# Shifting the SBUF addresses of matmul operands: distances of 64 and 96 bytes in place of 0 and 32

## The chip, the cores and the metric

The kernel runs on one core of a Trainium2 chip. TensorE (PE) multiplies; its weight loads are listed as PEld. VectorE (DVE), ScalarE (ACT) and GpSimd (POOL) do the elementwise work, and SyncE (SP) issues nearly all DMAs in order from one queue. The metric is device time in microseconds (us).

## The reference

Attention over pooled keys and values, and two gated MLP layers after it, all in float32:

```python
k_p = k.reshape(B, H, S//8, 8, D).mean(axis=3)      # B, H, S, D = 8, 8, 576, 64
v_p = v.reshape(B, H, S//8, 8, D).mean(axis=3)
attn = softmax(q @ k_p.T / sqrt(D)) @ v_p
x = attn                                            # as 4608 tokens x 512
h = x @ w_in                                        # 512 x 2048
x = (h * clip(h + 3, 0, 6) / 6) @ w_out             # first layer
g = x @ w_gate                                      # 512 x 1536
out = (g * sigmoid(g) * (x @ w_val)) @ w_out2       # second layer
```

## The kernel before

Every large product is computed from operands that are split into a high part (rounded to the type float32r) and a low part (the rest). Three matmuls, high x high, high x low and low x high, stand for one product of float32. Each matmul loads its own stationary operand: 128 columns of 4 bytes, 512 bytes in each partition. The next matmul's load runs beside the stream of the moving operand of the matmul before.

There are four large products, in this order of time:

- first layer, up (L623 in `mm3`, 1728 matmuls of 512 columns): moving `x`, stationary `wu`. It goes over nine blocks of 512 tokens and 16 slices of the weights, twelve matmuls each; between two such groups the matmuls of the next block's attention are put in (L424 to L604).
- first layer, down (L891 in `down_b`, 3024 matmuls of 256 columns): moving `gb`, stationary `pw`. It goes over nine blocks, and in each over seven products (a Strassen scheme: sums of quarters on VectorE, seven products in place of eight), 48 matmuls each.
- second layer, up (L712 in `mm3x`, called from `up2`, 3024 matmuls of 384 columns): moving `xc`, stationary `wr`. Six groups of 768 tokens, in each 12 slices of the weights with seven products.
- second layer, down (L712 from `down2`, 2268 matmuls of 256 columns): moving `wr`, stationary `gc`.

The weights of the second layer go through a ring of four buffers (`ring_tile`, tag `wr`), which SP fills by DMA in the order of use (L691 for up). Pools are given out in a stack from the left and one from the right of SBUF; where a new pool lies over the bytes of an old one, its first writer waits for the last users of the bytes. The order of all instructions is the order of the code.

The operands' addresses in a partition, in bytes, as the pools give them out, and their remainders modulo 256. All offsets inside these tiles, of slices that a matmul reads, are multiples of 256, so that the remainder of a tile is the remainder of each operand in it:

| Tile | Before | mod 256 | After | mod 256 |
|---|---|---|---|---|
| `wu`; `pw` of products 3 to 6 in the same pool | 17088 | 192 | 17088 | 192 |
| `x`; `pw` of products 2 and 7 in the same pool | 82624 | 192 | 82688 | 0 |
| `gb` | 115424 | 224 | 115456 | 0 |
| `px`: `pw` of product 1 | 178112 | 192 | 178112 | 192 |
| `xc` (its first pool; the others alike modulo 256) | 206816 | 224 | 206816 + 160 | 128 |
| `wr` (ring) | 161760 | 224 | 160224 + 64 | 32 |
| `gc` | 53952 | 192 | 53952 | 192 |

Moving minus stationary operand, modulo 256, is thus before 0 in both up products and 32 in both down products. After it is 64 in the first layer's up, 64 in five of the seven products of its down and 0 in the other two (products 2 and 7, whose `pw` lies in the pool of `x`), and 96 in both products of the second layer.

Of the kernel before, what the change touches and what calls it, by code (L numbers as in the profile page):

```python
# [8 lines left out]
F32 = mybir.dt.float32  # L9
F32R = mybir.dt.float32r  # L10
# [13 lines left out]
def kernel(  # L24
# [28 lines left out]
    P = 128  # L53
# [15 lines left out]

    left_b, l1, l1_ps = ExitStack(), ExitStack(), ExitStack()  # L70
    wu_p = left_b.enter_context(tc.tile_pool(name="wu", bufs=4))
    x_p = left_b.enter_context(tc.tile_pool(name="x", bufs=2))
    gap_p = left_b.enter_context(tc.tile_pool(name="gap", bufs=1))
    gb_p = left_b.enter_context(tc.tile_pool(name="gb", bufs=4))
    t_p = l1.enter_context(tc.tile_pool(name="t", bufs=2))
    ps_y = l1_ps.enter_context(tc.tile_pool(name="ps_y", bufs=1, space=PSUM))
# [6 lines left out]

    ident = const.tile([P, P], F32, name="ident")
    half = const.tile([P, 1], F32, name="half")
    gap_p.tile([P, 8], F32, name="gap")

    BIG = 4096

# [10 lines left out]
    M = 384  # L100
# [47 lines left out]
    def split(hi, lo, src, lo_engine):  # L148
        nc.scalar.copy(out=hi, in_=src)  # L149
        lo_engine.tensor_tensor(out=lo, in0=src, in1=f32(hi), op=ALU.subtract)  # L150
# [58 lines left out]
    def sums_b(eng, v, ops=("T1", "T3", "T2", "T4")):  # L209
        for what in ops:  # L210
            a, b = {"T1": ("12", "11"), "T3": ("22", "12"), "T2": ("22", "T1"), "T4": ("21", "T2")}[what]
            eng.tensor_tensor(out=v(what), in0=v(a), in1=v(b), op=ALU.subtract)
# [6 lines left out]
    def new_q7(name):  # L219
        return q7_p.tile([P, 8 * WH], F32R, tag="q7", name=name)  # L220
# [433 lines left out]
    l2 = {}  # L654
    xc, ys, gf, gc, wr = {}, {}, {}, {}, {}
# [10 lines left out]
    def x_step(p, n, lo_eng, sum_eng):  # L666

        t = ys[p]
        place = {"11": 0, "T1": 0, "12": 1, "T3": 1, "21": 2, "T4": 2, "22": 3, "T2": 3}
        v = lambda what: t[:, place[what]]  # L670
        what, then = [("11", "T1"), ("22", "T3"), ("T1", "T2"), ("T2", None), ("21", "T4"), ("T4", None), ("T3", None)][n]
        if what == "11":
            x = new_q7("xc")[:, :4 * M].rearrange("p (a k n) -> p a k n", a=2, k=2)
        else:
            pool = l2["xa" if what in ("T1", "22") else "xt" if what == "T3" else "xb"]
            x = pool.tile([P, 2, 2, M], F32R, tag="x" + what, name="xc")
        xc[p, what] = x
        split(x[:, 0], x[:, 1], v(what), lo_eng)
        if then:
            sums_b(sum_eng, v, (then,))  # L680

    def ring_tile():
        return l2["ring"].tile([P, 2048], F32R, tag="wr", name="wr")

    def load_up(u):

        f, m = u
        src = s_up[f][m].rearrange("p s a k f -> p s (a k f)")
        for h, (a, b) in enumerate(((0, HALF), (HALF, 7))):
            t = ring_tile()  # L690
            nc.sync.dma_start(  # L691
                out=f32(t[:, :512 * (b - a)]), in_=src[:, a:b].rearrange("p s n -> p (s n)")
            )
            for s in range(a, b):
                wr["up", u, s] = t[:, 512 * (s - a):512 * (s - a + 1)].rearrange("p (a k f) -> p a k f", a=2, k=2)

    def load_dn(n):
        s = B7[DN[n][2]]
        src = s_dn[:, s].rearrange("p f a n -> p (f a n)")
        for h in range(2):  # L700
            t = ring_tile()
            k = NPAIR // 2 * 512
            nc.sync.dma_start(out=f32(t[:, :k]), in_=src[:, k * h:k * (h + 1)])
            for f in range(NPAIR // 2):
                wr["dn", n, NPAIR // 2 * h + f] = t[:, 512 * f:512 * (f + 1)].rearrange("p (a n) -> p a n", a=2)
# [236 lines left out]
    for j in range(NB):  # L942
        t0 = j * N
        while t0 < (j + 1) * N:
            b, s0 = t0 // S, t0 % S
            n = min(S - s0, (j + 1) * N - t0)
# [198 lines left out]
    with tc.manual_schedule():  # L1145
# [105 lines left out]
        for i in range(7 * NB):  # L1251
            j, n = divmod(i, 7)
            down_b(i)
            for c in range(NCB):
                if c % (NCB // 2) == 0 and sums_at.get(n, ((), ()))[c // (NCB // 2)]:
                    sum_b(j, *sums_at[n][c // (NCB // 2)])
                split_b(i + 1, c)
            for slot in {3: (0,), 4: (2,), 5: (3, 1)}.get(n, ()):
                load_g(j + 1, slot)
            if j == NB - 1 and n >= 5:  # L1260
                if n == 5:
                    right_b.close()
                    prep_ctx.close()
                    for nm, bufs in (("xa", 1), ("ring", 4), ("xb", 1)):
                        l2[nm] = ctx.enter_context(
                            tc.tile_pool(name=nm, bufs=bufs, side="right", reuse_waits="tile"))
                load_next()
                for step in ((0,), (1, 2, 3))[n - 5]:
                    x_step(0, step, nc.vector, nc.vector)
            evac_b(j, n)  # L1270
            prep_slot(F1 * (NB - 1) + i)
            if (j, n) == (NB - 1, 3):
                assert not prep_at
                load_y(0)
        for step in (4, 5):
            x_step(0, step, nc.vector, nc.vector)
        for send in last_y:
            send()
        left_b.close()
        l2["xt"] = ctx.enter_context(tc.tile_pool(name="xt", bufs=1, side="right", reuse_waits="tile"))  # L1280
        x_step(0, 6, nc.vector, nc.vector)
        for nm, bufs in (("gf", 1), ("gc", 6), ("t", 1), ("o", 1)):
            l2[nm] = ctx.enter_context(tc.tile_pool(name=nm + "2", bufs=bufs, reuse_waits="tile"))
# [59 lines left out]
```

## Time and profile before

| What | Value |
|---|---|
| Median of three runs | 1747.0 us (1746.58 to 1748.53) |
| The profiled execution's own time | 1755.87 us |
| Its span (first to last instruction) | 1753.7 us |
| PE busy | 1698.7 us, 97% of the span |
| DVE busy | 1335.5 us, 76% |
| Granted TensorE clock, mean | 0.988 of full |

The profiled execution is one run with the profiler on; 2.2 us of its time lie outside the span, and it is 8.9 us above the median of the runs without a profile. Matmuls are pipelined: the duration of one record is longer than the distance from its start to the next one's start. Where matmuls follow each other with no idle time, a stretch of time divided by their number gives that distance.

### The profile page before, as it was taken

Reading aid. Unit: us, or ns where it says so; the run is one execution under the profiler, and the core shown is the slowest. Engines: PE = TensorE matmul, PEld = TensorE weight load, DVE = VectorE, ACT = ScalarE, POOL = GpSimd, SP = SyncE. Lnnn points to the kernel's source line nnn. Section 1 sums busy time; section 2 is a strip of 40 time slices with the busy share of each in tenths; the row PEclk is TensorE's granted clock in tenths of the full one; section 3 lists DMA queues with packets and bytes.
Section 4 is the critical chain, followed back from the end, with each engine's and each line's share of the span. In section 5 each row is a group of like instructions: output and inputs, shape, how many; then the busy total and the mean of one; then the engine's idle time right before and its main releaser. Section 6 shows DMA issues by size and latency. Waiting matters only on the chain.

```text
span 1753.7 us, 30755 instructions
## 1 busy us (share of the span) xinstructions
PE 1698.7 (97%) x11116; PEld 1603.2 (91%) x11116; DVE 1335.5 (76%) x2356; ACT 752.3 (43%) x1656; POOL 639.8 (36%) x821
## 2 busy tenths in 40 slices
PE   5789999999999999999999999999999999999999
PEld 4678887878788899999998999999999999999999
DVE  6797897888975578888887668668668668668666
ACT  5565554545544445555554224224224224224223
POOL 6555675656822000000000560560560560560560
PEclk8799999999999999999999999999999999999999
DMA  7666888888767974655554878878868878878776
GB/s 182 165 177 191 241 268 252 247 266 241 229 234 263 413 290 169 186 205 217 207 207 167 285 241 279 309 240 279 309 240 280 308 240 281 307 241 281 271 240 217
DMA packets 237784, 432.48 MB, mean 247 GB/s; under 512 B 87104, under 2 KB 169024, under 8 KB 220480
## 3 DMA queue, kind: packets, MB, share of 16 engines
q1 hardware_dynamic: 236576, 430.25, 73.6%
q8 instruction: 88, 1.44, 0.3%
q14 instruction: 64, 0.52, 0.1%
q10 hardware_dynamic: 1056, 0.26, 0.1%
HBM read 326.11 MB, written 104.33 MB: 245 GB/s over the span
## 4 chain that ended last, share of the span: by engine, by line
PE 83%; DMA 6%; DVE 6%; POOL 1%; ACT 1%; SPq 1%; issue 1%; DVEq 0%; POOLq 0%; ACTq 0%
PE b L712 45%; PE b L891 20%; PE h L623 14%; DMA g<-g 2%; DMA q_in<-in_q_dram 2%; PE pss L503 1%; DMA qv<-in_q_dram 1%; DVE g L638 1%; DMA y<-o 1%; SPq L384 1%; PE pst L573 1%; PE pst L577 0%; DVE vtl L469 0%; PE psv L601 0%; DVE qT L485 0%
## 5 line engine op out<-in xcount | busy, mean ns | idle before, releaser
L712 PE MATMUL b<-xc,wr 128*128 128x384 f32 x3024 | 527.9, 335 | 4.5 <-ACT xc L149 2.6
L712 PEld LDWEIGHTS b<-xc,wr 128*128 128x128 f32 x3024 | 525.5, 188 | 5.8 <-ACT xc L149 3.3
L623 PE MATMUL h<-x,wu 128*128 128x512 f32 x1728 | 432.6, 402 | 6.3 <-DVE g L638 6.1
L759 POOL TENSOR_TENSOR s<-s,c 128x384 f32<-128x384 f32 x144 | 142.3, 1013 | 755.3 <-ACT s L757 755.3
L721 DVE TENSOR_TENSOR c<-c,b 128x384 f32<-128x384 f32 x504 | 264.8, 552 | 174.6 <-PE b L712 149.8
L623 PEld LDWEIGHTS h<-x,wu 128*128 128x128 f32 x1728 | 321.5, 192 | 73.1 <-DVE g L638 8.8
L891 PEld LDWEIGHTS b<-gb,pw 128*128 128x128 f32 x3024 | 356.3, 188 | 0.2
L891 PE MATMUL b<-gb,pw 128*128 128x256 f32 x3024 | 356.4, 280 | 0.0
L712 PE MATMUL b<-wr,gc 128*128 128x256 f32 x2268 | 265.6, 279 | 0.0
L712 PEld LDWEIGHTS b<-wr,gc 128*128 128x128 f32 x2268 | 265.4, 188 | 0.0
L149 ACT CAST gb<-gq 128x512 fp32r<-128x512 f32 x252 | 155.3, 621 | 159.3 <-PE b L891 140.6
L150 DVE TENSOR_TENSOR gb<-gq,gb 128x512 fp32r<-128x512 f32 x252 | 167.5, 687 | 53.1 <-ACT gb L149 52.4
L766 POOL TENSOR_TENSOR gf<-s,c 128x384 f32<-128x384 f32 x144 | 168.2, 1192 | 66.3 <-DVE c L721 64.5
L149 ACT CAST gc<-gf 128x768 fp32r<-128x768 f32 x126 | 105.6, 838 | 187.1 <-POOL gf L766 100.8
L757 ACT ACTIVATE s<-c 128x384 f32<-128x384 f32 x144 | 73.4, 525 | 198.4 <-DVE c L721 197.1
L150 DVE TENSOR_TENSOR gc<-gf,gc 128x768 fp32r<-128x768 f32 x126 | 134.2, 1093 | 16.2 <-ACT gc L149 14.0
L634 ACT ACTIVATE g<-h,half 128x512 f32<-128x512 f32 x144 | 98.9, 687 | 78.6 <-PE h L623 62.8
L638 DVE SCALAR_TENSOR_TENSOR g<-g,h 128x512 f32<-128x512 f32 x144 | 97.4, 677 | 24.4 <-ACT g L634 24.3
L551 POOL TENSOR_TENSOR e<-e,sm 128x288 f32<-128x288 f32 (+4 forms) x74 | 48.3, 653 | 128.0 <-DVE sm L547 100.2
L729 ACT COPY c<-b 128x384 f32<-128x384 f32 x72 | 33.9, 470 | 127.4 <-PE b L712 127.4
L869 DVE TENSOR_TENSOR gq<-gq 128x1024 f32<-128x1024 f32 x72 | 87.7, 1218 | 0.0
L207 DVE TENSOR_TENSOR gf<-gf 128x768 f32<-128x768 f32 (+1 forms) x66 | 66.9, 1029 | 12.2 <-POOL gf L766 10.9
(101 smaller groups left out, 1660.1 us busy)
## 6 DMA issues: line engine op xcount, KB each, us to landing
wr<-sup SPq DMA_DIRECT2D x72, 1024.0 KB
wr<-sdn SPq DMA_DIRECT2D x84, 768.0 KB
wr<-sup SPq DMA_DIRECT2D x72, 768.0 KB
g<-g SPq DMA_DIRECT2D x144, 256.0 KB
gq<-g SPq DMA_DIRECT2D x36, 1024.0 KB
wstg<-in_moe_w_out_dram SPq DMA_DIRECT2D x56, 256.0 KB
pw<-sw SPq DMA_DIRECT2D x14, 1024.0 KB
sup<-s SPq DMA_DIRECT2D x12, 1024.0 KB
```

Of the source, the lines that this page charges most:

```text
L149: nc.scalar.copy(out=hi, in_=src)
L150: lo_engine.tensor_tensor(out=lo, in0=src, in1=f32(hi), op=ALU.subtract)
L623: nc.tensor.matmul(out=ps, lhsT=w(kt, wh), rhs=x(kt, xh), start=first and n == 0, stop=last and n == 3 * len(kts) - 1,)
L634: nc.scalar.activation(out=t, in_=ps, func=ACTF.Relu, bias=half, scale=1.0 / 6.0)
L638: nc.vector.scalar_tensor_tensor(out=t, in0=t, scalar=1.0, in1=ps, op0=ALU.min, op1=ALU.mult)
L712: nc.tensor.matmul(out=ps, lhsT=w(wh), rhs=x(xh), start=first and n == 0, stop=last and n == 2)
L721: add = lambda dst, a, b: nc.vector.tensor_tensor(out=dst, in0=a, in1=b, op=ALU.add)
L757: nc.scalar.activation(out=g[q], in_=c[q], func=ACTF.Sigmoid)
L759: nc.gpsimd.tensor_tensor(out=g[q], in0=g[q], in1=c[q], op=ALU.mult)
L766: nc.gpsimd.tensor_tensor(out=gf[p][:, GP[TURN[q]], f], in0=g[q], in1=c[q], op=ALU.mult)
L869: nc.vector.tensor_tensor(out=v(what), in0=v(a), in1=v(b), op=op)
L891: nc.tensor.matmul(out=ps[:, d], lhsT=w[:, CB * c + k, wh, P * d:P * (d + 1)], rhs=g[:, gh, k], start=what == place and (c, d, k, m) == (0 ...
```

## The change

It moves tiles by some bytes. The dummy tile `gap`, 32 bytes between the pool `x` and the pool `gb`, becomes 64 bytes between the pool `wu` and the pool `x`. In the second layer the tiles of `xc` and of the ring get 64 elements (256 bytes) more, and the operands start 40 and 16 elements (160 and 64 bytes) into them. No instruction is added or removed, and the engines' orders are the same.

```diff
     wu_p = left_b.enter_context(tc.tile_pool(name="wu", bufs=4))
+    gap_p = left_b.enter_context(tc.tile_pool(name="gap", bufs=1))
     x_p = left_b.enter_context(tc.tile_pool(name="x", bufs=2))
-    gap_p = left_b.enter_context(tc.tile_pool(name="gap", bufs=1))
     gb_p = left_b.enter_context(tc.tile_pool(name="gb", bufs=4))
...
-    gap_p.tile([P, 8], F32, name="gap")
+    gap_p.tile([P, 16], F32, name="gap")
...
         if what == "11":
-            x = new_q7("xc")[:, :4 * M].rearrange("p (a k n) -> p a k n", a=2, k=2)
+            x = new_q7("xc")
         else:
             pool = l2["xa" if what in ("T1", "22") else "xt" if what == "T3" else "xb"]
-            x = pool.tile([P, 2, 2, M], F32R, tag="x" + what, name="xc")
-        xc[p, what] = x
+            x = pool.tile([P, 4 * M + 64], F32R, tag="x" + what, name="xc")
+        x = xc[p, what] = x[:, 40:40 + 4 * M].rearrange("p (a k n) -> p a k n", a=2, k=2)
...
     def ring_tile():
-        return l2["ring"].tile([P, 2048], F32R, tag="wr", name="wr")
+        return l2["ring"].tile([P, 2048 + 64], F32R, tag="wr", name="wr")[:, 16:16 + 2048]
```

The longer tiles move the pools of the right side, and with them what some first writers of the second layer wait for. On SP, at the passage from the first layer to the second (`wr` is the ring, `sup` the prepared weights in memory, `ystg` and `y` the first layer's result, DVE_49 and the like are semaphores), the waits of the first four loads of weights change:

```order
 L663 DMA ystg<-y 128x2x384 [waits DMAHW3_49]
 L663 DMA ystg<-y 128x2x384 [waits DMAHW4_49]
-L691 DMA wr<-sup_107 128x2048 [waits DMAHW5_49,DVE_49]
+L691 DMA wr<-sup_107 128x2048 [waits DMAHW5_49,DVE_49,Activation_49]
 L691 DMA wr<-sup_107 128x1536 [waits PE_49]
-L691 DMA wr<-sup_108 128x2048
+L691 DMA wr<-sup_108 128x2048 [waits DVE_49]
 L691 DMA wr<-sup_108 128x1536 [waits DMAHW0_49]
 L912 DMA y<-o_11512 128x2x256 [waits DMAHW1_49,DVE_49]
```

Before, the first ring buffer covered the first 32 bytes of the quarter `gq` of slot 1, whose last reader is the last split of `gb` on DVE (L150); that wait moves to the third load. The first load now waits for the sum of L869 on DVE before it, and for a cast of ACT (L149) before it, which read the quarters that the buffer lies over now.

On ACT, at the same place, the third row is the cast that fills the last `xc` of the first group (`xt`), which lies over other buffers of the first layer's output than before:

```order
 L149 CAST xc<-ystg 128x768 [waits DMAHW3_49]
 L149 CAST xc<-ystg 128x768 [waits DVE_49]
-L149 CAST xc<-ystg 128x768 [waits DMAHW2_49,DMAHW1_49]
+L149 CAST xc<-ystg 128x768 [waits DMAHW2_49,DMAHW6_49,DMAHW1_49,DMAHW0_49]
 L729 COPY c_11620<-b 128x384 [waits PE_49]
```

It waits for two more stores of that output (L912), and the subtraction on DVE behind it for one more. Nothing else differs on any engine, PE among them.

## Rows read from the trace of the kernel before

**Rows 1.** The page's first part: the span, and each engine's busy time.

```profile
span 1753.7 us, 30755 instructions
PE 1698.7 (97%) x11116; PEld 1603.2 (91%) x11116; DVE 1335.5 (76%) x2356; ACT 752.3 (43%) x1656; POOL 639.8 (36%) x821
```

**Rows 2.** The chain that ended last: shares of the span by engine, by line.

```profile
PE 83%; DMA 6%; DVE 6%; POOL 1%; ACT 1%; SPq 1%; issue 1%; DVEq 0%; POOLq 0%; ACTq 0%
PE b L712 45%; PE b L891 20%; PE h L623 14%; DMA g<-g 2%; DMA q_in<-in_q_dram 2%; PE pss L503 1%; DMA qv<-in_q_dram 1%; DVE g L638 1%; DMA y<-o 1%; SPq L384 1%; PE pst L573 1%; PE pst L577 0%; DVE vtl L469 0%; PE psv L601 0%; DVE qT L485 0%
```

**Rows 3.** Groups of instructions: count | busy us, mean ns | idle before, releasers.

```profile
L712 PE MATMUL b<-xc,wr 128*128 128x384 f32 x3024 | 527.9, 335 | 4.5 <-ACT xc L149 2.6 <-DVE xc L150 1.1 <-DMA wr<-sup 0.7
L623 PE MATMUL h<-x,wu 128*128 128x512 f32 x1728 | 432.6, 402 | 6.3 <-DVE g L638 6.1
L891 PE MATMUL b<-gb,pw 128*128 128x256 f32 x3024 | 356.4, 280 | 0.0
L712 PE MATMUL b<-wr,gc 128*128 128x256 f32 x2268 | 265.6, 279 | 0.0
```

**Rows 4.** Windows by stage: each engine's busy us (count), clock, DMA share.

```profile
core 0: us, PE busy (x) PEld busy (x) DVE busy (x) ACT busy (x) POOL busy (x), PEclk, DMA share, GB/s
53.00:331.00 278.00, 263.88 (x1376) 220.99 (x1375) 228.42 (x507) 154.46 (x456) 170.78 (x266) 0.97 0.75 222
331.00:597.20 266.20, 258.32 (x1303) 214.25 (x1303) 203.10 (x451) 134.13 (x339) 130.16 (x203) 0.99 0.80 262
597.20:954.30 357.10, 356.43 (x3025) 356.07 (x3023) 306.00 (x433) 185.09 (x305) 0.00 (x0) 1.00 0.59 213
1093.00:1181.00 88.00, 88.00 (x513) 88.00 (x512) 56.22 (x96) 21.72 (x42) 48.79 (x47) 1.00 0.80 278
1181.00:1225.00 44.00, 44.00 (x376) 44.00 (x375) 38.34 (x52) 19.69 (x29) 2.97 (x2) 1.00 0.80 272
954.30:1749.90 795.60, 791.74 (x5292) 790.41 (x5292) 561.25 (x874) 247.66 (x418) 310.54 (x288) 1.00 0.78 271
```

**Rows 5.** Windows inside L712 up, L712 down and L891, columns as above.

```profile
1100.00:1170.00 70.00, 70.00 (x405) 70.00 (x404) 45.46 (x77) 16.48 (x32) 41.38 (x39) 1.00 0.80 278
1445.00:1485.00 40.00, 40.00 (x345) 40.00 (x344) 35.53 (x47) 19.17 (x28) 1.90 (x2) 1.00 0.77 266
700.00:900.00 200.00, 200.00 (x1701) 200.00 (x1699) 174.90 (x251) 106.12 (x176) 0.00 (x0) 1.00 0.56 195
```

**Rows 6.** Timeline of PE at the end of L623: start, length, count [idle before].

```profile
555.80 34.91 PE L623 MATMUL h<-x,wu 128*128 128x512 f32 x152
591.08 3.03 PE L623 MATMUL h<-x,wu 128*128 128x512 f32 x12 [0.37 <-DVE g L638]
```

**Rows 7.** A window at half the clock, inside L712 up.

```profile
958.60:961.80 3.20, 3.20 (x11) 3.20 (x11) 2.27 (x4) 0.83 (x1) 0.00 (x0) 0.50 0.98 297
```

**Rows 8.** Timeline at the passage to the second layer.

```profile
948.72 0.69 DVE L150 TENSOR_TENSOR gb<-gq,gb 128x512 fp32r<-128x512 f32 x1 [0.73 <-ACT gb L149]
949.44 2.24 SPq L691 DMA_DIRECT2D wr<-sup  x4
952.04 7.01 SPq L912 DMA_DIRECT2D y<-o  x3
954.36 1.30 PE L712 MATMUL b<-xc,wr 128*128 128x384 f32 x6 [0.73 <-DMA wr<-sup]
957.12 0.45 PE L712 MATMUL b<-xc,wr 128*128 128x384 f32 x1 [1.47 <-ACT xc L149]
958.12 5.87 PE L712 MATMUL b<-xc,wr 128*128 128x384 f32 x23 [0.55 <-DVE xc L150]
964.28 0.83 ACT L149 CAST xc<-ystg 128x768 fp32r<-128x768 f32 x1 [2.89 <-DMA y<-o]
965.16 0.45 PE L712 MATMUL b<-xc,wr 128*128 128x384 f32 x1 [1.18 <-ACT xc L149]
```

## Prediction

> **What bounds the kernel now.** I read the engines' busy time first. PE is busy in 97% of the span, DVE in 76% [rows 1]. The chain that ended last says the same by another way: 83% of it is PE, and 79% of it three lines, L712, L891 and L623 [rows 2]. These are the four large products, 10,044 matmuls. Their groups have next to no idle time: 4.5 us ahead of L712 up, 6.3 us ahead of L623, nothing ahead of the other two [rows 3]. So what counts is the distance in time from one matmul's start to the next one's, and the mean duration of a record (335 ns for L712 up) does not give it, since records overlap. The windows by stage show how close the others are: in the second layer PE is busy for 791.74 of 795.60 us, DVE for 561.25, and the DMA share is 0.78. The tightest places are L891, where DVE has 306.00 of 357.10 us, and L712 down with 38.34 of 44.00 [rows 4].
>
> Now the distance itself, from windows in which PE is never idle. I divide by the number of weight loads, less one that began before the window [rows 5]. L712 up: 70.00 us / 403 = 173.7 ns. L712 down: 40.00 / 343 = 116.6. L891: 200.00 / 1698 = 117.8. L623 from the timeline: 152 matmuls in 34.91 us, of which the last record (402 ns, [rows 3]) belongs to one: (34.91 - 0.40) / 151 = 228.5 ns [rows 6].
>
> What would a matmul take if nothing disturbed it? One stretch tells. In a window at a granted clock of 0.50, that is 1.2 GHz, eleven records of 384 columns, one of them begun before, fill 3.20 us: 320 ns each, exactly one column per cycle [rows 7]. At 2.4 GHz that is half: 213.3 ns for 512 columns, 160.0 for 384, 106.7 for 256. What is left over I call the excess:
>
> L623, distance 0: 15.2 ns. L712 up, distance 0: 13.7. L891, distance 32: 11.1. L712 down, distance 32: 9.9.
>
> All of it is 1728 x 15.2 + 3024 x 13.7 + 3024 x 11.1 + 2268 x 9.9 = 26.3 + 41.4 + 33.6 + 22.5 = 124 us, and it is the only thing the change can touch. Two facts in it matter. At half the clock, and at distance 0, the excess is nothing, though each matmul loads its weights there too. A fixed price of swapping weights, counted in cycles, would show there; reads that get in each other's way only when the moving operand is read at full rate would not. And the stages at distance 32 have 10.5 ns on average, those at 0 have 13.7 or more. The flaw of this comparison is that the stages at 32 also have 256 columns, and no stage has the same columns at both distances; also L891 and L712 down differ by 1.2 ns at the same distance.
>
> **The change part by part.** No instruction is added or removed, and PE's order is the same, so each term is a number of matmuls times a difference of excess. The excess at distances 64 and 96 stands in no row, so I bound it. From below: 0, as at half the clock. From above: the twelve matmuls that follow an idle 0.37 us took 3.03 us, (3.03 - 0.40) / 11 = 239.1 ns each [rows 6], 10.6 more than in the long run, which is the most that a row shows on top (the first load, which nothing hides, is in it). Between them I go by the one step that the rows have: 3.2 ns fewer from 0 to 32. I take it that each further step of 32 bytes brings half of the one before: 10.5 - 1.6 = 8.9 ns at 64 and 8.1 at 96. That is a choice. A straight line (7.3 and 4.1) is as simple, but it would leave nothing at 128, and the 1.2 ns between two stages at one distance says that part of the excess has another cause.
>
> - L623, 0 to 64: 13.7 - 8.9 = 4.8 ns x 1728 = 8.3 us. PE is idle here for 22 of 544 us, waiting for attention's steps on other engines [rows 4], so a faster PE waits a little more; I count 7.
> - L891, five products of seven, 32 to 64: 11.1 - 8.9 = 2.2 ns x 2160 = 4.8 us. DVE has 51 us to spare in the stage [rows 4]; that hides it.
> - L891, products 2 and 7, 32 back to 0: 13.7 - 11.1 = 2.6 ns x 864 = 2.2 us lost.
> - L712 up, 0 to 96: 13.7 - 8.1 = 5.6 ns x 3024 = 16.9 us. A window of L712 up has DVE at 56.22 of 88.00 us and DMA at 0.80 [rows 4]; two or three per cent more of that rate is to be had.
> - L712 down, 32 to 96: 9.9 - 8.1 = 1.8 ns x 2268 = 4.1 us, with 5.7 us of 44 left on DVE [rows 4]; without that rest the term would be 0.
>
> The moved waits come to nothing. Before, the first four loads of the second layer stood at SP's head until 949.44 us, just behind the last split on DVE, which ends at 949.41 [rows 8], and PE's first matmul waited 0.73 us for the first. Now that load waits for an earlier sum and cast, so it can land up to 4 us earlier; PE then starts 0.73 us earlier, and waits that much longer at 957.12, where it stood 1.47 us for ACT's cast of `xc`, whose chain does not depend on the loads. The wait has moved to the third load, which was issued after 949.44 anyway; behind it on SP stand one load and the stores of `y`, and none comes later. The cast at 964.28 waited 2.89 us for a store and now waits for two more; SP issues these in order, and I count 0, with 0.7 us as gain and 1 us as loss for the bounds.
>
> Sum: 7 + 4.8 - 2.2 + 16.9 + 4.1 = 30.6 us. The profiled execution's 1755.9 us would become 1725.3; it stands 0.5% above the median of the runs, 1747.0, which becomes 1747.0 - 30.4 = 1717.
>
> **A rule against it.** At half the clock the excess is nothing and at full clock 13.7 ns in L712 up [rows 5, 7]. The Trainium skill (TensorE: Matmul & The Clock Gate, "Step-by-step: what each phase is for") says that PE reads SBUF through two independent ports, and that "Loading the next tile's weights doesn't steal SBUF read bandwidth from the running matmul." By that sentence the gain would be 0, against the 30.6 us of the sum. The same page ("Back-to-back issue gap") gives columns / 2.4 + 2.5 ns for a warm matmul; by that estimate 162.5 ns would stand where the window shows 173.7, so the trace does not agree with it, and a gain could at most reach 112 - 9180 x 2.5 ns = 89 us.
>
> **The rivals.**
>
> *Nothing changes.* The excess belongs to something else than the addresses: to the number of columns, say, which parts the stages just as the distance does. For it: the confusion named above, and 1.2 ns of difference at equal distance. Against it: the excess vanishes at half the clock, which points to reads. Time: 1747, within 3.5 us (0.2%, about what a measurement of this kernel can tell from no change).
>
> *Far more goes.* The line is straight, or the operands keep clear of each other altogether. Straight: L623 6.4 ns (11.1 us, I count 9), L891 8.2 - 2.2, L712 up 9.6 ns (29.0), L712 down 5.8 ns (13.2): 57 us, 1690. To the lower bound of 0: 26.3 + 24.0 - 2.2 + 41.4 + 22.5 = 112 us, 1635. Then L712 down would need 40.3 us for what takes 44, and DVE's 38.34 there would be close to the bound, which speaks against the very end.
>
> *Slower.* The moving operand is read faster than the weights are loaded, so a distance at the start does not stay: the two streams meet again during a load if both return to the same place after 256 bytes. The start then only sets how often they meet, and 64 or 96 may bring one meeting more than 0 or 32. Place: every matmul of the four products. Price: one step of the row's size the wrong way, 3.2 ns x 9180 = 29.4 us, and the 2.2 us of products 2 and 7: 1779. With the upper bound of 10.6 ns: 97 + 2 us, 1846. It decides from 0.4 ns per matmul on, since 9180 x 0.4 ns = 3.7 us is past what can be told. For it: no row shows any distance beyond 32, and a falling line may well turn. Against it: the one step that is seen falls.
>
> **How the numbers follow.** The forecast with a gain of 4 to 40 us has 0.42, the larger gain 0.23, nothing 0.15, slower 0.20. Faster is 0.42 + 0.23 = 0.65. The forecast's own range is 1707 to 1743. For 8 in 10 I go down to the part of the larger gains that the straight line covers with some margin, 1672, which leaves out about 0.08, and up to 1755, which takes in nothing and the mildest of the slower cases and leaves out about 0.12.
>
> **What the changed profile would show.** The same windows decide each term: L712 up from 173.7 to about 168 ns, L712 down from 116.6 to 114.8, L891 117.8 to about 115.6 in products 1 and 3 to 6 and to some 120 in products 2 and 7, L623 from 228.5 to about 224. If the windows of L712 up stay at 173 to 174, nothing has changed; if they pass 174, the slower rival holds. The wait of 0.73 us for the first load should be gone and PE's wait for `xc` be longer by as much. The forecast is wrong if the excess depends on the columns, or if its fall turns before 64 bytes.

## The result, and the profile after

The changed kernel takes 1757.67 us (median of three, 1756.92 to 1761.59) against 1747.0 before. The ratio is 1.0053, with a 95% interval of 1.0031 to 1.0075: slower by 9.3 us (5 to 13). The forecast was 1717, its own range 1707 to 1743, and 1755 the upper end for 8 in 10.

The profiled execution hides this at first. Its span is 1754.9 us against 1753.7 [rows 1], only 1.2 us more. So the stages have to be read one by one. The windows by stage of the kernel after (columns as in [rows 4]):

```profile
core 0: us, PE busy (x) PEld busy (x) DVE busy (x) ACT busy (x) POOL busy (x), PEclk, DMA share, GB/s
53.00:589.00 536.00, 517.14 (x2675) 431.51 (x2675) 430.65 (x958) 288.80 (x793) 300.97 (x468) 0.99 0.78 244
589.00:939.60 350.60, 349.61 (x3026) 349.41 (x3025) 304.84 (x432) 185.39 (x304) 0.00 (x0) 1.00 0.61 221
939.60:1750.70 811.10, 808.21 (x5293) 807.63 (x5292) 562.90 (x874) 247.85 (x418) 311.38 (x288) 1.00 0.79 264
```

The second layer takes 811.1 us where it took 795.6: 15.5 us more, and PE is still busy for nearly all of it. L891 takes 350.6 where it took 357.1. The first stage takes 536 where it took 544, and that is no gain of faster matmuls, for they are not faster (below). The execution of before had a mean granted clock of 0.988, this one has 0.993. As the clock has two levels, 1.2 and 2.4 GHz, 2 x 0.012 x 1753.7 = 42 us of the one and 2 x 0.007 x 1754.9 = 25 us of the other were at the lower one: 17 us fewer. Some 7 of them lie ahead of the stage, since from 20 to 53 us the granted clock is 0.70 before and 0.80 after (2 x 0.10 x 33 = 6.6). The other 10 are worth up to 5 us, and PE is idle for 18.9 us of the stage in place of 22.0: together that is about the 8 us. The profiled execution of before also stood 8.9 us above its median, that of after 0.8 us below its own.

The groups of instructions of the kernel after (busy us, mean ns of one record, idle time before):

```profile
L712 PE MATMUL b<-xc,wr 128*128 128x384 f32 x3024 | 537.2, 339 | 2.9 <-ACT xc L149 2.3
L623 PE MATMUL h<-x,wu 128*128 128x512 f32 x1728 | 428.9, 400 | 5.2 <-DVE g L638 5.1
L891 PE MATMUL b<-gb,pw 128*128 128x256 f32 x3024 | 349.7, 278 | 1.0 <-DMA pw<-sw 1.0
L712 PE MATMUL b<-wr,gc 128*128 128x256 f32 x2268 | 273.1, 282 | 0.0
```

Against [rows 3], both products of the second layer are up (527.9 to 537.2, 265.6 to 273.1), L891 is down (356.4 to 349.7), and nowhere has a wait grown that would explain it: idle time ahead of L712 has fallen from 4.5 to 2.9 us. It is the matmuls themselves. Windows inside L712 up and L712 down, where [rows 5] had 173.7 and 116.6 ns:

```profile
1090.00:1160.00 70.00, 70.00 (x398) 70.00 (x397) 45.35 (x77) 15.71 (x30) 39.59 (x37) 1.00 0.79 269
1170.00:1210.00 40.00, 40.00 (x336) 40.00 (x335) 35.84 (x47) 19.23 (x28) 2.21 (x2) 1.00 0.79 260
```

By the same count (weight loads less one) that is 70.00 / 396 = 176.8 and 40.00 / 334 = 119.8 ns. And weight loads alone in three windows of L891: in product 1 of the first block (distance 64), in product 2 of a later block (0), in its products 3 to 6 (64). Here and in all such rows below the columns are the window, its length, PEld's busy time (number of loads), the granted clock, the DMA share and GB/s:

```profile
589.20:594.20 5.00, 5.00 (x44) 1.00 1.01 416
751.80:756.80 5.00, 5.00 (x43) 1.00 0.05 18
758.00:778.00 20.00, 20.00 (x178) 1.00 0.46 145
```

20.00 / 177 = 113.0 ns at 64 and 5.00 / 42 = 119 at 0; the first window, at 64 too, has 5.00 / 43 = 116. Short windows are coarse. The mean distance of all starts in the trace, taken product by product, is 113.3 ns at 64 from the second block on, 117.8 in four of the five such products of the first block, and 120.0 at 0. That one distance has two times is taken up below. L623, timeline of PE at its end:

```profile
542.37 46.86 PE L623 MATMUL h<-x,wu 128*128 128x512 f32 x204
```

(46.86 - 0.40) / 203 = 228.9 ns, against 228.5 [rows 6]: nothing gained at 64.

At half the clock the change makes no difference in L712 up. A window in the kernel after, at distance 96 (window, PE's busy time and records, clock, DMA share, GB/s):

```profile
944.30:947.50 3.20, 3.20 (x11) 0.50 0.46 163
```

It holds the same eleven records in 3.20 us as the window at distance 0 before [rows 7], 320 ns each.

The passage to the second layer went as the orders said. Timeline of the kernel after:

```profile
932.13 4.14 SPq L691 DMA_DIRECT2D wr<-sup  x3
938.07 7.01 SPq L912 DMA_DIRECT2D y<-o  x3
939.61 1.22 PE L712 MATMUL b<-xc,wr 128*128 128x384 f32 x6
943.16 0.44 PE L712 MATMUL b<-xc,wr 128*128 128x384 f32 x1 [2.33 <-ACT xc L149]
944.15 8.15 PE L712 MATMUL b<-xc,wr 128*128 128x384 f32 x36 [0.55 <-DVE xc L150]
```

PE no longer waits for the first load (0.73 us before, [rows 8]), and the wait for ACT's cast has grown from 1.47 to 2.33 us.

### The profile page after: what moved, and what is told of

The parts are those of the page before. It is cut to its first block, busy times and chain, and to the rows that moved or that the text cites. A ratio compares the mean times of both kernels' runs of the same rounds, so it can differ in the third digit from the quotient of the medians.

```text
span 1754.9 us, 30757 instructions
## 1 busy us (share of the span) xinstructions
PE 1702.3 (97%) x11116; PEld 1609.2 (92%) x11116; DVE 1335.9 (76%) x2356; ACT 753.4 (43%) x1656; POOL 641.3 (37%) x821
## 4 chain that ended last, share of the span: by engine, by line
PE 81%; DMA 7%; DVE 7%; ACT 1%; issue 1%; POOL 1%; SPq 1%; DVEq 0%; POOLq 0%; ACTq 0%
PE b L712 46%; PE b L891 19%; PE h L623 12%; DMA pw<-sw 2%; PE pss L503 1%; DVE g L638 1%; DMA qv<-in_q_dram 1%; DMA g<-g 1%; DMA wstg<-in_moe_w_out_dram 1%; DVE s L278 1%; DMA wstg<-in_moe_w_in_dram 1%; DMA k_in<-in_k_dram 1%; DVE mx L513 1%; DMA gq<-g 1%; DVE qT L485 1%
## 5 line engine op out<-in xcount | busy, mean ns | idle before, releaser
L712 PE MATMUL b<-xc,wr 128*128 128x384 f32 x3024 | 537.2, 339 | 2.9 <-ACT xc L149 2.3
L712 PEld LDWEIGHTS b<-xc,wr 128*128 128x128 f32 x3024 | 535.4, 188 | 3.5 <-ACT xc L149 2.7
L623 PE MATMUL h<-x,wu 128*128 128x512 f32 x1728 | 428.9, 400 | 5.2 <-DVE g L638 5.1
L623 PEld LDWEIGHTS h<-x,wu 128*128 128x128 f32 x1728 | 318.8, 190 | 70.7 <-DVE g L638 6.5
L891 PE MATMUL b<-gb,pw 128*128 128x256 f32 x3024 | 349.7, 278 | 1.0 <-DMA pw<-sw 1.0
L891 PEld LDWEIGHTS b<-gb,pw 128*128 128x128 f32 x3024 | 349.5, 189 | 1.2 <-ACT gb L149 1.2
L712 PE MATMUL b<-wr,gc 128*128 128x256 f32 x2268 | 273.1, 282 | 0.0
L712 PEld LDWEIGHTS b<-wr,gc 128*128 128x128 f32 x2268 | 272.8, 188 | 0.0
L149 ACT CAST gb<-gq 128x512 fp32r<-128x512 f32 x252 | 155.5, 621 | 152.7 <-PE b L891 106.1
L150 DVE TENSOR_TENSOR gb<-gq,gb 128x512 fp32r<-128x512 f32 x252 | 167.5, 688 | 47.7 <-ACT gb L149 46.7
L149 ACT CAST gc<-gf 128x768 fp32r<-128x768 f32 x126 | 105.6, 838 | 194.8 <-POOL gf L766 103.2
L150 DVE TENSOR_TENSOR gc<-gf,gc 128x768 fp32r<-128x768 f32 x126 | 133.9, 1092 | 21.7 <-ACT gc L149 20.1
L869 DVE TENSOR_TENSOR gq<-gq 128x1024 f32<-128x1024 f32 x72 | 87.8, 1219 | 0.0
L207 DVE TENSOR_TENSOR gf<-gf 128x768 f32<-128x768 f32 (+1 forms) x66 | 66.9, 1029 | 12.1 <-POOL gf L766 10.8
```

The costliest lines, as they stand in the source:

```text
L623: nc.tensor.matmul(out=ps, lhsT=w(kt, wh), rhs=x(kt, xh), start=first and n == 0, stop=last and n == 3 * len(kts) - 1,)
L712: nc.tensor.matmul(out=ps, lhsT=w(wh), rhs=x(xh), start=first and n == 0, stop=last and n == 2)
L869: nc.vector.tensor_tensor(out=v(what), in0=v(a), in1=v(b), op=op)
L891: nc.tensor.matmul(out=ps[:, d], lhsT=w[:, CB * c + k, wh, P * d:P * (d + 1)], rhs=g[:, gh, k], start=what == place and (c, d, k, m) == (0 ...
```

## The experiments

In all of them only addresses are moved, and with them some waits. The times in ns are mean distances between starts of neighbouring matmuls of one product in the profiled execution, at the full clock, without the gaps above 40 ns more than the columns take.

**The two halves of the change.** The first kernel has the edits of the pools `gap`, `x` and `wu` alone, the second those of `xc` and the ring alone.

```diff
     wu_p = left_b.enter_context(tc.tile_pool(name="wu", bufs=4))
+    gap0_p = left_b.enter_context(tc.tile_pool(name="gap0", bufs=1))
     x_p = left_b.enter_context(tc.tile_pool(name="x", bufs=2))
-    gap_p = left_b.enter_context(tc.tile_pool(name="gap", bufs=1))
     gb_p = left_b.enter_context(tc.tile_pool(name="gb", bufs=4))
...
-    gap_p.tile([P, 8], F32, name="gap")
+    gap0_p.tile([P, 16], F32, name="gap0")
```

> The first layer's part of the change alone: 64 in its up product, 64 and 0 in its down product; the second layer as before (0 and 32). Theory A (the time of a matmul depends on the distance modulo 256, with a curve of its own for each number of columns): L891 at 113.8 ns in five products and 120 in products 2 and 7, L623 about 0.6 ns slower than before, L712 back at 173.4 and 116.7. Sum: 2160 x 4.0 - 864 x 2.3 - 1728 x 0.6 = 5.6 us less than before, 1741. Rival B (the loss in the changed kernel is not in the matmuls but in the waits at the passage between layers): L712's windows as before but the total near 1757.

Measured: ratio 0.9976 (0.996 to 0.9992), 4.2 us less than before (1.4 to 7). L891 113.4 ns at 64 and 120.0 at 0, L623 229.7 (229.0 before), L712 173.4 and 116.7.

> The second layer's part alone: 96 in both of its products; the first layer as before (0 and 32). Theory A: L712 up at 176.6 ns and down at 120.0, so 3024 x 3.3 + 2268 x 3.3 = 17.5 us more than before, 1764. Rival B (waits, not matmuls): no more than 3 us from before.

Measured: ratio 1.006 (1.0044 to 1.0075), 10.5 us more (8 to 13). The groups of the two kernels, first the half in the first layer, then the half in the second:

```profile
L712 PE MATMUL b<-xc,wr 128*128 128x384 f32 x3024 | 529.3, 335 | 5.2 <-ACT xc L149 2.3 <-DMA wr<-sup 2.1 <-DVE xc L150 0.9
L891 PE MATMUL b<-gb,pw 128*128 128x256 f32 x3024 | 349.1, 278 | 0.8 <-DMA pw<-sw 0.8
L712 PE MATMUL b<-wr,gc 128*128 128x256 f32 x2268 | 265.6, 279 | 0.0
```

```profile
L712 PE MATMUL b<-xc,wr 128*128 128x384 f32 x3024 | 537.2, 339 | 3.0 <-ACT xc L149 2.5 <-DVE xc L150 0.6
L891 PE MATMUL b<-gb,pw 128*128 128x256 f32 x3024 | 353.2, 279 | 0.0
L712 PE MATMUL b<-wr,gc 128*128 128x256 f32 x2268 | 273.1, 282 | 0.0
```

So the first layer's half is a gain and the second's a loss, each in its own stage, and the groups are those of the whole change to within 0.6 us: rival B is out. The product of the two ratios, 1.0036, lies in the interval of the whole. The 10.5 us are less than the 17.5 expected; the groups of L712 are 16.8 us longer than in [rows 3], but L891, whose addresses are those of before, is 3.2 us shorter in this execution (116.7 ns in place of 117.7). That leaves 13.6 us, and what the rest is stays open. A window of L891 in it, over the same stretch as in [rows 5]:

```profile
700.00:900.00 200.00, 200.00 (x1715) 1.00 0.56 199
```

200.00 / 1714 = 116.7 ns, against 117.8 there. So the distance 32 has two times as well. The profiled execution of before has both: 116.7 in the first two products of L891, 117.8 in all that follow.

**All distances in steps of 32 bytes.** Each of six kernels gives each product another distance, with gaps between the pools (for 160 to 224 in L623, `x` stands before `wu`), another padding behind `px`, and other offsets in `xc` and the ring. The first of them against the kernel before:

```diff
     wu_p = left_b.enter_context(tc.tile_pool(name="wu", bufs=4))
+    gap0_p = left_b.enter_context(tc.tile_pool(name="gap0", bufs=1))
     x_p = left_b.enter_context(tc.tile_pool(name="x", bufs=2))
...
-    gap_p.tile([P, 8], F32, name="gap")
+    gap_p.tile([P, 16], F32, name="gap")
+    gap0_p.tile([P, 8], F32, name="gap0")
...
-            x = pool.tile([P, 2, 2, M], F32R, tag="x" + what, name="xc")
-        xc[p, what] = x
+            x = pool.tile([P, 4 * M + 64], F32R, tag="x" + what, name="xc")
+        x = xc[p, what] = x[:, 24:24 + 4 * M].rearrange("p (a k n) -> p a k n", a=2, k=2)
...
-        return l2["ring"].tile([P, 2048], F32R, tag="wr", name="wr")
+        return l2["ring"].tile([P, 2048 + 64], F32R, tag="wr", name="wr")[:, 8:8 + 2048]
```

> Distances: L623 32, L891 96 (products 1, 3 to 6) and 64 (products 2 and 7), L712 up 64, L712 down 64. Theory A: at 256 columns 64 gives 113 to 115 ns and 96 about 120, in either layer and at other addresses than in the changed kernel. Theory C (one curve for all numbers of columns): L712 up at 64 falls by 4 ns below its 173.4 as well, to 169.5, and L623 at 32 falls by 2 ns. Theory D (the address of one operand modulo 256 counts, not the distance): products 2 and 7 of L891, at the same distance 64 but with both operands 32 bytes further, do not come to 113.8.

> Distances: L623 96, L891 128 (products 1, 3 to 6) and 32 (products 2 and 7), L712 up 32, L712 down 0. Theory A: L891 at 32 gives 117.8 again though both operands stand elsewhere, L712 down at 0 about 120. Theory C: L712 up at 32 gives 2 ns less than its 173.4. Theory D: L891 at 32 is away from 117.8 by more than 1 ns.

> Distances: L623 128; L891 160 in product 1, 0 in products 2 and 7, 128 in the others; L712 up 128, down 128. Theory A (256 bytes is the period, each number of columns has its own curve): 128 need not be like 0. Theory E (the period is 128 bytes): as at 0, that is 120 ns at 256 columns, 173.3 at 384, 227 to 229 at 512. The run with 128 in L891 gave 118.7 already, which speaks for A.

> Distances: L623 160; L891 224 in product 1, 128 in 2 and 7, 32 in 3 to 6; L712 up 160, down 160. Theory E: as at 32, that is 116.7 to 117.8 ns at 256 columns, 173.9 at 384, 233 at 512. Theory A: other values; below the time at 0 somewhere if there is a best distance beyond 96.

> Distances: L623 192; L891 192 in product 1, 128 in 2 and 7, 64 in 3 to 6; L712 up 192, down 192. Theory E: as at 64, 113.3 or 117.8 ns at 256 columns, 173.3 at 384, 229.7 at 512. Theory A: other values. Theory G (two states at one distance, and the products before decide which): 64 in L891 after a stretch at 128, not at 0, does not reach 113.3 but stays near 117.8.

> Distances: L623 224; L891 0 in product 1, 96 in 2 and 7, 64 in 3 to 6; L712 up 224, down 224. Theory E: as at 96, 120.0 ns at 256 columns, 176.7 at 384. Theory G: 64 in products 3 to 6 comes after 96 here and stays at 117.8, as it did after 96 before. Theory D (an operand's own remainder counts): product 1 at distance 0 with remainders 32 and 32 would not come to 120.0.

What each sets (gaps in bytes between the three pools of the left side, padding of `px` and offsets of `xc` and `wr` in elements):

| Kernel | Left side | `px` | `xc`, `wr` |
|---|---|---|---|
| 1 | `wu` 32 `x` 64 `gb` | 8 | 24, 8 |
| 2 | `wu` 96 `x` 32 `gb` | 8 | 0, 56 |
| 3 | `wu` 128 `x` 0 `gb` | 16 | 56, 24 |
| 4 | `x` 96 `wu` 32 `gb` | 32 | 8, 32 |
| 5 | `x` 64 `wu` 64 `gb` | 24 | 24, 40 |
| 6 | `x` 32 `wu` 64 `gb` | 48 | 40, 48 |

Single runs, in this order: 1756.15, 1764.21, 1762.24, 1751.5, 1752.33 and 1750.25 us; the first two beside runs of before with a median of 1750.33, the others beside one at 1744.58. None is faster than the kernel before, as each holds several worse distances at once. The matmuls, in ns, with the kernels before and after, the halves and those of the next part put in (where two times are given, executions or stretches of one execution have the one or the other):

| Distance | L623, 512 columns | L712 up, 384 | L891, 256 | L712 down, 256 |
|---|---|---|---|---|
| 0 | 229.0 | 173.4 | 119.8 to 120.0 | 120.0 |
| 32 | 233.2 | 173.3, or 176.7 | 116.7, or 117.8 | 116.7 |
| 64 | 229.7 | 173.3 | 113.3, or 117.8 | 117.8 |
| 96 | 233.6 | 176.7 | 120.0 | 120.0 |
| 128 | 232.4 | 175.9 | 118.7 | 118.9 |
| 160 | 234.1 | 173.4 | 117.5 | 117.3 |
| 192 | 233.3 | 174.7, or 176.7 | 113.3, or 117.8 | 113.3, or 117.8 |
| 224 | 233.0 | 173.4 | 118.3 | 118.3 |

The second layer goes over its six groups of tokens one after the other. In the second kernel L712 up at 32 has the longer time in the first group alone; in the fifth, both of its products at 192 change from group to group. Weight loads of the second kernel in the first and the second group of L712 up, then of the fifth in the first and the second group of L712 down:

```profile
975.00:1045.00 70.00, 70.00 (x398) 1.00 0.80 271
1100.00:1170.00 70.00, 70.00 (x405) 1.00 0.83 285
```

```profile
1043.00:1083.00 40.00, 40.00 (x341) 1.00 0.78 264
1176.00:1216.00 40.00, 40.00 (x355) 1.00 0.78 267
```

70.00 / 397 = 176.3 and 70.00 / 404 = 173.3 ns; 40.00 / 340 = 117.6 and 40.00 / 354 = 113.0. Over all six groups the means are 173.9 at 32, and 175.7 and 115.6 at 192. The 118.9 at 128 is such a mean too: 120.0 in the first group of L712 down, 118.7 in the others. Whether the groups' own buffers play a part in that is not shown.

Some of the groups behind it: L712 up at 128 in the third of these kernels, and L712 down at 192 and L623 at 192 in the fifth (its lines stand two further on):

```profile
L712 PE MATMUL b<-xc,wr 128*128 128x384 f32 x3024 | 535.1, 339 | 2.9 <-ACT xc L149 2.3 <-DVE xc L150 0.5
```

```profile
L625 PE MATMUL h<-x,wu 128*128 128x512 f32 x1728 | 437.8, 405 | 4.6 <-DVE g L640 4.6
L714 PE MATMUL b<-wr,gc 128*128 128x256 f32 x2268 | 263.1, 279 | 0.0
```

535.1 against 527.9 us and 263.1 against 265.6 say the same as the means of 175.9 against 173.4 ns and of 115.6 against 116.7, within what waits and the clock add.

The table says this. The distance counts and not an operand's own remainder: 0 gives 119.8 to 120.0 at 256 columns with both operands at 0, at 32, at 64 or at 192 (theory D is out). The test that the first kernel was to be for D, 64 with both operands 32 bytes further, came out as D has it, 117.8 ns and not 113.8; but the next part shows both times at one pair of addresses, so that this test decides nothing. Each number of columns has its own curve (C is out): at 512 columns nothing is better than 0, at 384 nothing better than 0 by more than 0.1 ns, and only at 256 columns is 0 the worst together with 96. The period is not 128 bytes (E is out): at 512 columns 128 costs 3.4 ns more than 0. And at 96, the distance that the change gives the second layer, both of its products stand at the top of their columns, in each of the six groups of both profiled executions that have it (after, and the second half); no run shows a shorter time there. Theory G, that what runs ahead decides between two times at 64, held in the fifth kernel (117.8 ns after products at 128) and failed in the sixth (after a product at 96 it has 117.8 ns in the first block and 113.3 in the other eight, where the first kernel had 117.8 throughout).

**One distance, two times.** L891 at 64 had 113.3 ns in some executions and 117.8 in others. Four kernels leave L623 and L712 up at 0 and change L891. The first widens the old gap (`[P, 8]` to `[P, 16]`, in its old place): 64 throughout. The second adds to this that product 1 of each seven stands at 0:

```diff
-                    new_pw(0, lb["px"].tile([P, BIG + 8], F32R, tag="px", name="pw")[:, :BIG])
+                    new_pw(0, lb["px"].tile([P, BIG + 56], F32R, tag="px", name="pw")[:, :BIG])
```

The third puts the pool of `gb` ahead of `wu`, with 64 bytes between them, and pads `px` likewise: 192 throughout. The fourth has L712 down at 192 as well (`xc` and the ring both moved by 40 elements).

> Only L891 is changed, to 64 in all seven products; 0, 0 and 32 elsewhere as before. If one distance has one time (theory A alone), L891 falls to 113.5 ns throughout: 3024 x 3.2 to 4.2 = 10 to 13 us less than before, 1735 to 1740. Theory G (two states at 64, 113.4 and 117.8 ns, and what runs ahead decides): all of L891 in one of the two, or first in one and then in the other; in the slow one no gain, or 3 us lost.

Measured: 1.0008 (0.9993 to 1.0022), no gain. 117.8 ns in all of L891 in the profiled execution.

> As the one before, but product 1 of each seven at distance 0. Theory G: the stretch at 0 (120 ns each, locked) leads into the fast state at 64, so product 1 has 120 and the other six 113.4 ns in every block: 2592 x 3.2 to 4.2 - 432 x 2.2 to 3.3, 7 to 10 us less than before, 1738 to 1742, and faster than the kernel with 64 throughout if that one falls into the slow state. Theory A alone: slower than it by 432 x 6.5 = 2.8 us.

Measured: 0.9961 (0.9948 to 0.9974), 6.8 us less, twelve runs from 1738.69 to 1753.25. But the profiled execution is the slowest of the twelve and has 117.8 ns in the six products at 64: the stretch at 0 did not lead into the shorter time there.

> L891 at 192 in all seven products, the others at 0, 0 and 32. 192 gave 113.4 ns in product 1 of each block, after a stretch at 128 each time. If 192 leads into the fast state from anywhere: 113.4 throughout, 1735 to 1740. Theory G: 113.4 or, as L712 down at 192 has it in part, 117 to 119.

Measured: 0.9949 (0.993 to 0.9968), 8.9 us less. The profiled execution changes from one of the two times to the other within L891, in its fifth block of nine, and never back. Its weight loads, in a window before that and in one after:

```profile
600.00:740.00 140.00, 140.00 (x1190) 1.00 0.63 228
760.00:930.00 170.00, 170.00 (x1502) 1.00 0.56 197
```

140.00 / 1189 = 117.7 ns, then 170.00 / 1501 = 113.3, with the same instructions at the same addresses. The change stands where PE waited for DVE:

```profile
754.40 3.80 PE L891 MATMUL b<-gb,pw 128*128 128x256 f32 x31 [0.34 <-DVE gb L150]
```

Not every such wait brings one: in the kernel with 0 and 64, one of 0.27 us in the sixth block left the 117.8 ns as they were.

> As the one before, and L712 down at 192 as well, L712 up at 0 with both operands 32 bytes before a multiple of 160 moved alike. L712 down: 115.6 as at 192 before, 2268 x 1.1 = 2.5 us less than the one before; 173.4 ns in L712 up (theory D, one operand's remainder, would have it elsewhere).

Measured: 0.9968 (0.9945 to 0.9991). Its twelve runs fall into two groups, 1731.79 to 1736.58 (four) and 1744.89 to 1752.76 (eight). The profiled one is in the upper group, with 117.8 ns in L891 and in L712 down. L712 up has 173.4.

Then the same programs again, and one more with 128 in product 1 (`BIG + 40`) and 192 in the other six:

> The kernel with 192 in both down products once more, whose twelve runs fall into 1731.8 to 1736.6 (four) and 1744.9 to 1752.8 (eight). Theory G: if this run is in the lower group its L891 has 113.4 ns, if in the upper 117.8; 3024 x 4.4 = 13 us is the distance of the groups.

Measured: 1748.47 us, L891 at 117.8: the upper group, as the theory says. No execution of the lower group was profiled.

> The kernel with 0 in product 1 and 64 in the other six once more. In its profiled execution (1753.3 us) the six had 117.8 ns. Theory G: a run near 1741 shows 113.4 in them at the same addresses and the same order.

Measured: 1742.05 us. Weight loads of the six products at 64 in one block, first of the earlier profiled execution (1753.25 us), then of this one:

```profile
757.00:783.00 26.00, 26.00 (x223) 1.00 0.35 110
```

```profile
754.00:784.00 30.00, 30.00 (x266) 1.00 0.46 156
```

26.00 / 222 = 117.1 and 30.00 / 265 = 113.2 ns: one program, two times. Over the whole stage the means are 117.8 and 113.8, since the first block of the second execution still has the longer time. With 2592 such matmuls this is 10.4 us between the two executions, whose times differ by 11.2.

> The kernel with 64 throughout L891 once more; its twelve runs show no group below 1746. If 64 without a product at another distance never leaves the slow state: 117.8 ns again.

Measured: 1745.64 us; 115.2 ns on average: 117.8 in the first product, then 113.3 into the sixth block, then 117.8 to the end. Two windows, before and after the second change:

```profile
620.00:780.00 160.00, 160.00 (x1413) 1.00 0.60 208
800.00:920.00 120.00, 120.00 (x1020) 1.00 0.55 196
```

160.00 / 1412 = 113.3 and 120.00 / 1019 = 117.8 ns. So 64 throughout does leave the 117.8 ns at times; the expectation failed. Here too each change stands at a pause: two starts lie 222 ns apart at the first and 202 ns at the second.

> L891 at 128 in product 1 and at 192 in the other six; 0, 0 and 32 elsewhere. Where 192 followed a stretch at 128 it had 113.4 ns in all nine blocks. If 128 leads into the fast state: products 2 to 7 at 113.4 in every block and every run, 432 x 118.7 + 2592 x 113.4, 8 to 10 us less than before with little scatter, near 1740. If the state is chance: two groups of runs, as with 192 throughout.

Measured: 0.9958 (0.9938 to 0.9977), 7.3 us less, and eight runs within 1737.48 to 1742.53. In the profiled execution, products 2 to 7 of the first block and of the fifth:

```profile
605.00:632.00 27.00, 27.00 (x230) 1.00 1.01 424
754.00:784.00 30.00, 30.00 (x266) 1.00 0.47 155
```

27.00 / 229 = 117.9 and 30.00 / 265 = 113.2 ns: the first block keeps the longer time, the other eight have 113.4. This is one profiled execution; that the shorter time comes in every run is judged from the scatter of the eight alone. Five kernels are faster than before by intervals that do not reach 1: the first layer's half alone, 0 and 64, 192 throughout, 192 in both layers, and this one. I would choose the last: it is not clearly faster than 192 throughout (0.9949), but its runs scatter by 5 us where that one's scatter by 12.

## Why the prediction was wrong

*What was right.* The excess hangs on the distance between the operands, and it is there at the full clock only: at 1.2 GHz a matmul of 384 columns takes 320 ns at distance 0 and at 96. The passage between the layers cost nothing, and its waits moved as said. L891 came out on the side foretold, by more than foretold: the five products fell by 4.0 ns where 2.2 were counted (2160 x 4.0 = 8.6 us in place of 4.8), and products 2 and 7 rose by 2.3 where 2.6 were counted (2.0 us in place of 2.2). That these came so near is in part luck: the 13.7 ns counted at distance 0 came from 384 columns, and the 117.7 of before is the longer of two times at 32.

*The step that failed* is this one: "I take it that each further step of 32 bytes brings half of the one before: 10.5 - 1.6 = 8.9 ns at 64 and 8.1 at 96." It made one falling curve for all four products out of two products at 0 and two at 32 that differed in their columns too. The prediction called that the flaw of the comparison and went on all the same. The runs put a table in its place. At 256 columns the time falls from 0 over 32 to 64, though at 64 not always, and is back at the top at 96. At 384 it does not fall at all between 0 and 64 and is 3.3 ns higher at 96. At 512 it is 4.2 ns higher at 32 and as good as 0 at 64. So the first of the prediction's two signs of being wrong came true: the excess depends on the columns. Its 1.2 ns between two stages at one distance were the two times at 32, for L891 has 116.7 ns too, as L712 down has. The terms, as counted and as measured in the profiles before and after:

| Product | Counted | Measured |
|---|---|---|
| L623, 0 to 64 | -7 us | +0.7 ns x 1728 = +1.2 us |
| L891, 32 to 64 | -4.8 | -8.6 |
| L891, 32 to 0 | +2.2 | +2.0 |
| L712 up, 0 to 96 | -16.9 | +3.3 ns x 3024 = +10.0 |
| L712 down, 32 to 96 | -4.1 | +3.3 ns x 2268 = +7.5 |
| Sum | -30.6 | +12.1 |

The measured sum lies in the interval of the times, 5 to 13 us. It holds for these two executions: with L891 at 116.7 ns before, its two terms would be -6.5 and +2.9, and the sum +15.1.

*The rivals.* The slower one had the size, 3.2 ns per matmul against 3.3, but not the place: it holds in the second layer and not in the first, so that its 1779 us were too many. Whether the cause is its own, one more meeting of the two streams in a load, no run here shows. Far more goes had one product right: the straight line left 7.3 ns of excess at 64, and L891 has 113.7 - 106.7 = 7.0 there. Nothing-changes is out: at 256 columns the same instructions take 116.7 or 117.8 ns at 32, 120.0 at 0 and 113.3 or 117.8 at 64. The sentence of the Trainium skill (TensorE: Matmul & The Clock Gate, "Step-by-step: what each phase is for"), that loading the next weights takes nothing from the running matmul, does not agree with these runs: at the same columns and the same clock, a matmul's time follows the place of the weights relative to the moving operand. The formula that the prediction took from the same page of the Trainium skill ("Back-to-back issue gap") stands there for a matmul by itself; in a stream with a weight load for each matmul, as here, that section lets the matmul and the load together set the distance. So the 173.7 ns do not speak against it, and the 89 us that were worked out from it are no bound here.

## What to carry to other kernels

Before an address is moved, the time of a matmul has to be measured at that distance and with that number of columns; a curve from one shape does not hold for another. A mean over a whole stage can hide that two times take turns in it, so it is worth taking the mean by block. Eight distances for four products took six runs, because each run can test one distance in each stage. Where the runs of one program scatter by more than their waits explain, the distance between starts in each stage of two executions shows whether a stage has two times; then the scatter, and not the median alone, is what a change of layout should be judged by.

## What the hardware showed that was not expected

At a fixed distance a stream of matmuls settles at one time per matmul, and there can be two of them. With 256 columns they are 113.3 and 117.8 ns at 64 and 192 bytes, and 116.7 and 117.8 at 32; with 384 columns, 173.3 and 176.7 at 32 and 174.7 and 176.7 at 192. With 256 columns, both occur in one program at the same addresses (64 and 192), and within one execution. In the two executions that change at one distance of 64 or 192, each change stands at a pause between two starts (694, 222 and 202 ns), and other pauses bring none; in that of before, at 32, it stands between two products, with no pause.

Which of the two it is changed from run to run in some kernels (twelve runs in groups of four and eight, 13 us apart, of which only the upper one was profiled). At 192 with a product at 128 ahead it was the shorter one in eight of nine blocks of the last kernel; at 64 with a product at 128 ahead it was the longer one in all nine of the fifth of the six. A product at 0 ahead does not settle it: 113.3 ns followed in two kernels, from the second block on, and in one of two executions of a third. No run shows what tips it.
